# Tiles 6 and 7 split on ScalarE and VectorE, first logits two steps later, a fourth staging place for the second weight matrix

## The chip, the cores and the metric

One core of one Trainium2 chip runs the whole program. The metric is the device time of one execution in microseconds (us). The engines are named as in the profile: PE (matmul), PEld (weight load), DVE (VectorE), ACT (ScalarE), POOL (GpSimd), SP (SyncE, which here only issues transfers; its queue is SPq).

## The reference, cut to what matters

```python
x = attention(q, k, v)               # 4 batches, 8 heads, 768 positions, head size 64; ALiBi bias,
                                     # window of 96 positions plus 8 global ones, softmax
x = x.transpose(0, 2, 1, 3).reshape(3072, 512)
h = x @ w_in                         # 512 -> 2048
x = (h * sigmoid(h)) @ w_out         # 2048 -> 512
logits = x @ phi                     # 512 -> 32 slots
d = softmax(logits, axis=0)          # over the 3072 tokens
slot_out = relu((d.T @ x) @ w1) @ w2 # 8 experts, 4 slots each
out = softmax(logits, axis=1) @ slot_out
```

The weights `w_in` and `w_out` arrive as 64-bit words and are narrowed on the chip.

## The kernel before, in words

The 3072 tokens are 24 tiles of 128, and three tiles make a chunk (8 chunks). Matmuls run in float16 with each operand split into a high and a low half (`hi`, line 196, writes the rounded high half; `lo`, line 206, the remainder), so a product takes three matmuls. A `hi` on ACT or POOL is a copy with scale (L200, L202). A `lo` is a subtraction of two SBUF operands on DVE or POOL (L208) or a scaled one on DVE (L210).

Attention of a tile T is `load` (its q, k, v), `split` (hi and lo of q, k and v), four `s_step` (two heads each: scores by L316 or L326, bias and minimum by L331 on DVE, exp by L332 on ACT; after the second and the fourth, the probabilities of four heads are split and transposed by a DMA, L349) and two `pv_step` (L371, normalization L382 to L384, split and transposition of the result, L394). Tiles 0 to 5 are "paired": their q and k are used in float32, and only v and the probabilities are split. Tiles 6 and up split q, k and v as well. Which engine does a `hi` is read from strings indexed by tile: `HE` (q, k, v) and `PHE` (probabilities), and `PLE` for the `lo` of the probabilities; a tile beyond the string's end takes POOL for these. Loads of q, k and v of tiles 6 and up go through one staging set, `stage_m`, so the load of tile T+1 waits until the split of tile T has read it.

The dense part of a chunk is 16 `l1_step` (12 matmuls L503 to L505, tanh on ACT L507, gate on DVE L509, hi on ACT and lo on DVE) and, for the chunk's three tiles, the second product (L523 to L525) into three PSUM banks, `l2_end` (hi, lo and a DMA transposition L536) and `logits` (L545, then L547 to L551), queued a number of steps later by `at`. A "step" is one call of `slot_end`, about one `l1_step`. While chunk c is worked on, the attention items of the next chunk's tiles are dealt out over its steps: chunk 0 runs beside the attention of tiles 3 to 5 and the beginning of tile 6, with the splits of tiles 6, 7 and 8.

The weights come in 16 pieces of 1 MB, 0 to 7 of `w_in` and 8 to 15 of `w_out`. `w_ahead` (line 447) issues the load of the next piece as soon as its place in `place` is free; `conv` (line 454) narrows a piece and splits it: L461 on ACT, L463 on DVE, a check by two matmuls L468 (and L470 on ACT for every second piece), L471 on DVE, hi L481 on ACT, lo L489 on DVE; then its place is free. Pieces 10 to 15 are converted inside the second product of chunk 0, which needs piece 8 + i for its steps 2i and 2i + 1. The place of piece 11 is that of 8, of 12 that of 9, of 13 that of 10, of 14 that of 11, of 15 that of 12.

The text of the program is the priority order from which a scheduler makes each engine's fixed order; an engine, and SPq too, works strictly in its order.

Of the kernel before, what the change touches and what calls it, by code (L numbers as in the profile page):

```python
# [81 lines left out]

START = [3, 9, 14, 18, 22, 99, 99, 99]
AHEAD = [0, 0, 0, 0, 0, 5, 8, 11, 13, 15]
HE = 'AAAAAA'
PHE = 'AAAAAA'
PLE = 'VVVVVV'
LOE = 'VVVVVVVVVVVVVVVV'
BE = 'P'
NPAIR = 6  # L90
# [4 lines left out]
GATE = {1: (0, 0), 2: (0, 1), 3: (1, 0), 4: (1, 1), 5: (2, 0), 6: (2, 1)}  # L95
# [5 lines left out]
def fast_kernel(tc, keepp, q_l, k_l, v_l, q_f, k_f, n_global, n_local, w_in, w_out, phi, w1, w2, shapes, pick_c, out):  # L101
# [8 lines left out]
    with ExitStack() as ctx:  # L110
# [129 lines left out]
        def at(lag, fn):  # L240
            seq[0] += 1
            heapq.heappush(heap, (now[0] + lag, seq[0], fn))
# [195 lines left out]

        wq = [wo0 + 8192 * i for i in range(4)]
        we = [ext0, ext0 + 8192]  # L440
        place = [wq[0], wq[1], wq[2], wq[3], we[0], we[1], wq[0], wq[1], we[0], we[1], wq[3], we[0], we[1], wq[3], we[0], we[1]]
        holder = {}
        nload = [0]

        done_p = set()

        def w_ahead():
            while nload[0] < 16 and holder.get(place[nload[0]]) is None and (GATE.get(nload[0]) is None or GATE[nload[0]] in done_p):
                p = nload[0]
                holder[place[p]] = p  # L450
                nc.sync.dma_start(out=ar.view(place[p], [2048], I32), in_=(w_in if p < 8 else w_out)[p % 8].bitcast(I32))
                nload[0] += 1
# [74 lines left out]
        def l2_end(c, m):  # L527
            op = bW[(turn[0] + m) % 4]
            T = first[c] + m
            xh, xtr = x2hl[m], x2t[T % 3]  # L530
            hi("A", xh[:, 0], op, E_X2 - E_G - E_WO)
            lo("V", xh[:, 1], op, E_X2 - E_G - E_WO, xh[:, 0])
            if m == 0:
                absmax(6 + 2 * c, xh[:, 0, 0:128])
                absmax(7 + 2 * c, g_of[CHUNKS[c]][:, 15, 0, 0:128])
            nc.sync.dma_start_transpose(out=xtr, in_=xh.rearrange("p z f -> p (z f)"))  # L536
            at(6 if c == 0 else CFG["lag_l"], lambda: logits(c, m))


        def logits(c, m):  # L540
# [290 lines left out]
        for c in range(NCH):  # L831
# [11 lines left out]
                    st["d"] += 1  # L843

            for f in range(16):
                while nconv < len(AHEAD) and AHEAD[nconv] <= f:
                    conv(nconv)
                    nconv += 1
                l1_step(c, f)
                slot_end()  # L850
                if c == NCH - 1 and 1 <= f < 11:
                    w1_halves(1, False)
                elif c == NCH - 1 and f >= 14:
                    w1_halves(1)
            if c == NCH - 1:
# [12 lines left out]
                g_slot = [[g0 + 8192 * i for i in range(3) if min(4, -(-8192 * (i + 1) // (4 * per_f))) == q + 1] for q in range(4)]  # L868
                g_slot[3] += [g0 + 8192 * i for i in range(3) if 8192 * (i + 1) > 16 * per_f and g0 + 8192 * i not in g_slot[3]]
            if c == 0:  # L870
                for f in range(0, 16, 2):
                    if nconv < 16:
                        conv(nconv)
                        nconv += 1
                    for m in range(n):
                        l2_part(c, m, range(f, f + 2))
                    slot_end()
                    if f % 4 == 2:
                        slot_end()

                V.tensor_reduce(out=odd, in_=oddp, axis=AX.X, op=ALU.max)
                G.memset(acc, 0.0)
                G.memset(ssum, 0.0)
                G.memset(mrun[0], -3e38)
                absmax(4, wih[:, 0, 0, 0:128])
                absmax(5, woh[:, 0, 0, 0:128])
                absmax(NSMP - 1, phi16[:, :, 0], AX.XY)
                for m in range(n):
                    l2_end(c, m)
                    tick()  # L890
            elif c == NCH - 1:
                while heap:
                    tick()
                last_begin(c)
                pick = ar.view(ls0 + 512, [2, NS], F32)
                nc.sync.dma_start(out=pick, in_=pick_c.rearrange("p (s o c) -> p s o c", s=2, o=4)[:, :, 0])
                for q in range(3):
                    for f in range(4 * q, 4 * q + 4):
                        for j in range(4):
                            last_part(c, j, (f,))  # L900
                        w1_halves(1 + (f % 4 < 2))
                    w_units([wo0 + 8192 * q] + g_slot[q])
                for j in range(4):
                    last_part(c, j, range(12, 16))
                    last_end(c, j)
                    if j < 3:
                        last_turn(c, j)
                    if j in (1, 2):
                        w1_halves(1)
                w_units([home[1, 15]])  # L910
                for u in range(16):
                    home[1, u] = moved[u]
            else:
                for m in range(n):
                    for q in range(4):
                        l2_part(c, m, range(4 * q, 4 * q + 4))
                        if q == 3:
                            l2_end(c, m)
                        slot_end()
# [464 lines left out]
```

## Time and profile before

| what | value |
|---|---|
| median of 3 runs | 723.83 us (721.11 to 727.09) |
| profiled execution | 723.92 us |
| its span, first to last instruction | 722.1 us |
| PE busy | 672.4 us (93%), 5175 matmuls |
| DVE busy | 500.4 us (69%) |
| ACT busy | 357.3 us (49%) |
| POOL busy | 252.4 us (35%) |
| mean granted PE clock | 0.98 of full |

Busy shares are means over stages. A row of the timeline gives start, duration, engine, line, operation, output and inputs, and in brackets the idle time of that engine just before with what ended it. Matmul durations overlap, so their pace is read from start to start.

### The profile page before, as it was taken

The page shows a single profiled execution, that of the slowest core. Times are in us where ns is not written, and L with a number is a line of the kernel's source. Part 1 is how long each engine was busy: PE and PEld are TensorE (multiplying, and loading weights), DVE is VectorE, ACT ScalarE, POOL GpSimd, SP SyncE. Part 2 cuts the span into 40 slices and gives each one's busy share as a digit, 9 for nine tenths or more (in the row PEclk, how much of TensorE's full clock was granted, in tenths as well). Part 3 has the DMA queues.
Part 4 walks back from the last instruction along what each step waited for, and adds up shares of the span by engine and source line. Part 5 has one row for each costly group of instructions (what it writes and reads, how often), then busy time and mean ns, then how long its engine had stood idle before and what let it go on. Part 6 is the DMA issues. An engine that isn't in the chain of part 4 may idle for free.

```text
span 722.1 us, 13677 instructions
## 1 busy us (share of the span) xinstructions
PE 672.4 (93%) x5175; PEld 387.1 (54%) x5175; DVE 500.4 (69%) x1189; ACT 357.3 (49%) x902; POOL 252.4 (35%) x211
## 2 busy tenths in 40 slices
PE   4779989789999999999999999999999989999992
PEld 2445534346655665566556655665566536665552
DVE  4999998977854877387638873876386158797432
ACT  5678766436522553265235533652266147574322
POOL 3110103423552566235625662356143400190000
PEclk9989998999999999999999999999999999999997
DMA  7999657672482567536645566355424893196998
GB/s 222 242 296 265 188 153 236 182 174 59 118 161 59 117 133 167 96 80 123 141 84 117 121 156 118 74 119 116 74 42 65 200 293 106 61 369 241 389 401 293
DMA packets 165257, 120.08 MB, mean 166 GB/s; under 512 B 143936, under 2 KB 150464, under 8 KB 159168
## 3 DMA queue, kind: packets, MB, share of 16 engines
q1 hardware_dynamic: 163968, 118.15, 62.2%
q10 hardware_dynamic: 1216, 0.99, 0.4%
q8 instruction: 42, 0.69, 0.4%
q14 instruction: 31, 0.25, 0.1%
HBM read 79.01 MB, written 6.29 MB: 118 GB/s over the span
## 4 chain that ended last, share of the span: by engine, by line


## 5 line engine op out<-in xcount | busy, mean ns | idle before, releaser
L202 POOL TENSOR_SCALAR arena<-arena 128x1024 f16<-128x1024 f32 (+5 forms) x115 | 118.1, 1038 | 293.4 <-ACT arena L332 112.8
L503 PE MATMUL bank<-rows,arena 128*128 128x384 f16 x512 | 167.9, 329 | 0.0
L505 PE MATMUL bank<-rows,arena 128*128 128x384 f16 x512 | 167.7, 328 | 0.0
L504 PE MATMUL bank<-rows,arena 128*128 128x384 f16 x512 | 167.7, 328 | 0.0
L200 ACT ACTIVATE arena<-bank 128x384 f16<-128x384 f32 (+1 forms) x153 | 77.2, 505 | 156.4 <-DVE bank L509 92.5
L332 ACT ACTIVATE arena<-arena 128x256 f32<-128x256 f32 (+1 forms) x192 | 92.4, 482 | 86.8 <-DVE arena L331 85.6
L524 PE MATMUL bank<-arena 128*128 128x512 f16 x336 | 128.6, 383 | 2.3 <-DVE arena L489 2.3
L525 PE MATMUL bank<-arena 128*128 128x512 f16 x336 | 128.6, 383 | 0.0
L523 PE MATMUL bank<-arena 128*128 128x512 f16 x336 | 127.3, 384 | 0.5 <-DVE arena L210 0.5
L210 DVE SCALAR_TENSOR_TENSOR arena<-bank,arena 128x384 f16<-128x384 f32 (+2 forms) x154 | 87.6, 570 | 27.3 <-ACT arena L200 26.3
L208 POOL TENSOR_TENSOR arena<-arena 128x1024 f16<-128x1024 f32 (+1 forms) x45 | 93.4, 2077 | 25.1 <-ACT arena L200 22.1
L331 DVE CUSTOM_DVE_ANT_0 arena<-bank,arena 128x256 f32<-128x256 f32 (+1 forms) x192 | 70.3, 394 | 33.7 <-PE bank L326 29.8
L509 DVE SCALAR_TENSOR_TENSOR bank<-arena,bank 128x384 f32<-128x384 f32 x128 | 71.0, 558 | 26.3 <-ACT arena L507 25.3
L208 DVE TENSOR_TENSOR arena<-arena 128x1024 f16<-128x1024 f32 (+2 forms) x50 | 68.9, 1378 | 13.1 <-POOL arena L202 12.4
L210 DVE SCALAR_TENSOR_TENSOR arena<-arena 128x1024 f16<-128x1024 f32 (+3 forms) x64 | 66.7, 1057 | 8.8 <-POOL arena L202 5.7
L505 PEld LDWEIGHTS <-arena 128*128 128x128 f16 x512 | 50.3, 98 | 33.7 <-issue 0.7
L503 PEld LDWEIGHTS <-arena 128*128 128x128 f16 x512 | 50.2, 98 | 33.3 <-issue 5.6
L507 ACT ACTIVATE arena<-bank 128x384 f32<-128x384 f32 x128 | 61.5, 481 | 12.3 <-PE bank L505 11.5
L504 PEld LDWEIGHTS <-arena 128*128 128x128 f16 x512 | 50.3, 98 | 28.1 <-issue 0.7
L200 ACT ACTIVATE arena<-arena 128x1024 f16<-128x1024 f32 (+1 forms) x61 | 55.4, 913 | 15.3 <-DVE arena L210 8.2
L525 PEld LDWEIGHTS <-arena 128*128 128x128 f16 x336 | 33.1, 98 | 41.8 <-issue 3.6
L524 PEld LDWEIGHTS <-arena 128*128 128x128 f16 x336 | 33.2, 99 | 36.7 <-issue 3.5
(185 smaller groups left out, 817.1 us busy)
## 6 DMA issues: line engine op xcount, KB each, us to landing
arena<-in_w_dram SPq DMA_DIRECT2D x31, 1024.0 KB, 8.6
arena<-in_q_l_dram SPq DMA_DIRECT2D x18, 512.0 KB, 3.7
arena<-in_k_l_dram SPq DMA_DIRECT2D x18, 512.0 KB, 4.3
arena<-in_w_in_dram SPq DMA_DIRECT2D x8, 1024.0 KB, 6.0
arena<-in_w_out_dram SPq DMA_DIRECT2D x8, 1024.0 KB, 5.4
arena<-in_v_l_dram SPq DMA_DIRECT2D x24, 256.0 KB, 3.1
out_dram<-arena SPq DMA_DIRECT2D x4, 768.0 KB, 8.1
arena<-in_q_f_dram SPq DMA_DIRECT2D x6, 256.0 KB, 5.1
```

Source lines behind the costliest of these rows:

```text
L200: A.activation(out=out, in_=in_, func=AF.Copy, scale=p2(e))
L202: G.tensor_scalar(out=out, in0=in_, scalar1=p2(e), scalar2=0.0, op0=ALU.mult, op1=ALU.add)
L208: (V if eng == "V" else G).tensor_tensor(out=out, in0=in_, in1=h, op=ALU.subtract)
L210: return V.scalar_tensor_tensor(out=out, in0=in_, scalar=p2(e), in1=h, op0=ALU.mult, op1=ALU.subtract)
L332: A.activation(out=pw, in_=pw, func=AF.Exp, scale=-1.0, bias=nmx[:, T, h:h + 1], accum_out=psum_[T % 2][:, h:h + 1])
L503: mm(hp, wh, x[:, 0, k], start=(k == 0), stop=False)
L504: mm(hp, wh, x[:, 1, k], start=False, stop=False)
L505: mm(hp, wl, x[:, 0, k], start=False, stop=(k == 3))
L509: gated.append(V.scalar_tensor_tensor(out=hp, in0=th, scalar=1.0, in1=hp, op0=ALU.add, op1=ALU.mult))
L523: mm(op, gh, woh[:, f, 0], start=(f == 0), stop=False)
L524: mm(op, gh, woh[:, f, 1], start=False, stop=False)
L525: mm(op, gl, woh[:, f, 0], start=False, stop=(f == 15))
```

## The change

It makes four edits. `HE` becomes 8 long and `PHE` and `PLE` 7: the hi of q, k and v of tiles 6 and 7 and the hi of tile 6's probabilities go from POOL to ACT, the lo of tile 6's probabilities from POOL to DVE. In `l2_end`, the logits of chunk 0 are queued 8 steps later instead of 6. In `place`, piece 9 goes to `wq[2]`, and the pieces after it use the four places `we[0]`, `we[1]`, `wq[2]`, `wq[3]`: piece 11 takes the place of 5, 12 that of 8, 13 that of 10, 14 that of 11, 15 that of 12. And `most` bounds the pieces loaded: 9 at first, one more before steps 3, 5, 7, 9 and 11 of chunk 0, and all from its second product on.

```diff
-HE = 'AAAAAA'
-PHE = 'AAAAAA'
-PLE = 'VVVVVV'
+HE = 'AAAAAAAA'
+PHE = 'AAAAAAA'
+PLE = 'VVVVVVV'
...
-        place = [wq[0], wq[1], wq[2], wq[3], we[0], we[1], wq[0], wq[1], we[0], we[1], wq[3], we[0], we[1], wq[3], we[0], we[1]]
+        place = [wq[0], wq[1], wq[2], wq[3], we[0], we[1], wq[0], wq[1], we[0], wq[2], wq[3], we[1], we[0], wq[3], we[1], we[0]]
...
-        nload = [0]
+        nload, most = [0], [9]
...
-            while nload[0] < 16 and holder.get(place[nload[0]]) is None and (GATE.get(nload[0]) is None or GATE[nload[0]] in done_p):
+            while nload[0] < most[0] and holder.get(place[nload[0]]) is None and (GATE.get(nload[0]) is None or GATE[nload[0]] in done_p):
...
-            at(6 if c == 0 else CFG["lag_l"], lambda: logits(c, m))
+            at(8 if c == 0 else CFG["lag_l"], lambda: logits(c, m))
...
             for f in range(16):
+                if c == 0 and f in (3, 5, 7, 9, 11):
+                    most[0] += 1
+                    w_ahead()
...
             if c == 0:
+                most[0] = 16
```

The scheduler rebuilds every engine's order from about the sixth `l1_step` of chunk 0 to the middle of chunk 1; behind that the orders are the same. Three places matter below. The first is SPq at the end of chunk 0. In the kernel before (L451 loads pieces 14 and 15; L268 loads q, k, v of tile 8, then q and k of tile 9; the two L349 of 128x8x128 transpose tile 6's probabilities):

```order
L451 DMA arena<-in_w_out_dram 128x2048
L349 DMA_TRANSPOSE arena<-arena 128x16x128
L268 DMA arena<-in_q_l_dram 128x1024
L451 DMA arena<-in_w_out_dram 128x2048
L349 DMA_TRANSPOSE arena<-arena 128x8x128
L268 DMA arena<-in_k_l_dram 128x1024
L268 DMA arena<-in_v_l_dram 128x512
L394 DMA_TRANSPOSE rows<-arena 128x8x128
L268 DMA arena<-in_q_l_dram 128x1024
L349 DMA_TRANSPOSE arena<-arena 128x8x128
L268 DMA arena<-in_k_l_dram 128x1024
```

In the changed kernel, from piece 14 to the first transpositions of `l2_end` (L536):

```order
L451 DMA arena<-in_w_out_dram 128x2048
L349 DMA_TRANSPOSE arena<-arena 128x16x128
L451 DMA arena<-in_w_out_dram 128x2048
L349 DMA_TRANSPOSE arena<-arena 128x8x128
L268 DMA arena<-in_q_l_dram 128x1024
L268 DMA arena<-in_k_l_dram 128x1024
L268 DMA arena<-in_v_l_dram 128x512
L394 DMA_TRANSPOSE rows<-arena 128x8x128
L268 DMA arena<-in_k_l_dram 128x1024
L268 DMA arena<-in_v_l_dram 128x512
L536 DMA_TRANSPOSE arena<-arena 128x8x128 x2
```

The load of tile 9's k now stands right behind tile 5's last transposition (L394) and ahead of the L536, and the second transposition of tile 6's probabilities, which stood ahead of it, is behind the L536.

The second place is ACT in the first steps of the second product. Before (L461 and L481 are conversions, L332 the exp of tile 5):

```order
L332 ACTIVATE arena<-arena 128x256 x2
L481 ACTIVATE arena<-arena 128x2x512
L470 ACTIVATE arena<-bank_77 128x512
L332 ACTIVATE arena<-arena 128x256
L461 ACTIVATE arena<-arena 128x1024
```

In the changed kernel (the three L200 are the hi of q, k and v of tile 7, the two L481 are pieces 10 and 11):

```order
L332 ACTIVATE arena<-arena 128x256 x2
L200 ACTIVATE arena<-arena 128x1024
L200 ACTIVATE arena<-arena 128x8x128
L200 ACTIVATE arena<-arena 128x8x64
L470 ACTIVATE arena<-bank_77 128x512
L481 ACTIVATE arena<-arena 128x2x512 x2
```

Three hi of tile 7 now stand in front of the check of piece 11 and of the hi of pieces 10 and 11.

The third place is DVE around the last conversion. Before (L489 is the lo of piece 15, L208 of 64x1024 the lo of tile 8's q, the two L208 of 128x8x128 the lo of k of tiles 8 and 9, the L210 from banks 73 to 75 the lo of `l2_end`, L509 the first gate of chunk 1):

```order
L331 ISA arena<-bank_71,arena 128x128
L331 ISA arena 128x1
L208 TENSOR_TENSOR arena<-arena 64x1024
L489 SCALAR_TENSOR_TENSOR arena<-arena 128x2x512
L208 TENSOR_TENSOR arena<-arena 128x8x128
...
L210 SCALAR_TENSOR_TENSOR arena<-bank_74,arena 128x512
L210 SCALAR_TENSOR_TENSOR arena<-bank_75,arena 128x512
L208 TENSOR_TENSOR arena<-arena 128x8x128
L509 SCALAR_TENSOR_TENSOR bank_76<-arena,bank_76 128x384
```

In the changed kernel:

```order
L208 TENSOR_TENSOR arena<-arena 128x8x128
L489 SCALAR_TENSOR_TENSOR arena<-arena 128x2x512
...
L210 SCALAR_TENSOR_TENSOR arena<-bank_74,arena 128x512
L208 TENSOR_TENSOR arena<-arena 128x8x128
L210 SCALAR_TENSOR_TENSOR arena<-bank_75,arena 128x512
L210 SCALAR_TENSOR_TENSOR arena<-arena 128x8x64
L509 SCALAR_TENSOR_TENSOR bank_76<-arena,bank_76 128x384
L331 ISA arena<-bank_71,arena 128x128
L331 ISA arena 128x1
L331 ISA arena<-bank_71,arena 128x128
L331 ISA arena 128x1
L208 TENSOR_TENSOR arena<-arena 64x1024
```

Two scores of tile 6 (L331 from bank 71) and the lo of tile 8's q went behind the last conversion and behind chunk 1's first gate; the lo of tile 8's k went ahead of the conversion, and that of tile 9's k ahead of the third lo of `l2_end`.

## Rows read from the trace of the kernel before

**Rows 1.** Busy time by stretch: busy us (instructions) per engine, PE clock, DMA, GB/s.

```profile
100.85:151.40 50.55, 44.28 (x256) 19.51 (x255) 48.34 (x73) 26.52 (x56) 18.34 (x12) 0.93 0.71 208
109.20:115.60 6.40, 6.40 (x16) 2.17 (x16) 6.40 (x11) 2.17 (x6) 3.71 (x2) 0.50 0.77 273
162.65:170.00 7.35, 7.35 (x50) 4.35 (x50) 4.58 (x17) 4.88 (x16) 3.18 (x2) 0.77 0.12 38
170.00:231.00 61.00, 61.00 (x469) 35.32 (x467) 36.98 (x98) 24.64 (x73) 26.40 (x20) 1.00 0.52 110
```

**Rows 2.** Waits of PE, 100 to 170 us: total, times, longest.

```profile
PE bank L545 <- DVE arena L548: 2.7, 1, 2.7
PE bank L524 <- DVE arena L489: 2.3, 3, 1.5
PE bank L468 <- DVE arena L463: 1.7, 3, 0.8
PE bank L316 <- DVE arena L331: 1.7, 1, 1.7
PE bank L523 <- DVE arena L210: 0.5, 1, 0.5
```

**Rows 3.** Timeline of DVE: instructions with two SBUF inputs, two plain ones first.

```profile
89.51 0.68 DVE L208 TENSOR_TENSOR arena<-arena 128x512 f16<-128x512 f32 x1
146.58 1.23 DVE L489 SCALAR_TENSOR_TENSOR arena<-arena 128x1024 f16<-128x1024 f32 x1
...
96.02 2.06 DVE L208 TENSOR_TENSOR arena<-arena 128x1024 f16<-128x1024 f32 x1
113.53 1.78 DVE L489 SCALAR_TENSOR_TENSOR arena<-arena 128x1024 f16<-128x1024 f32 x1
128.56 1.52 DVE L489 SCALAR_TENSOR_TENSOR arena<-arena 128x1024 f16<-128x1024 f32 x1
130.00 2.17 DVE L471 SCALAR_TENSOR_TENSOR arena<-arena 128x1024 int32<-128x1024 int32 x1
133.23 1.52 DVE L210 SCALAR_TENSOR_TENSOR arena<-arena 128x512 f16<-128x512 f32 x1
```

**Rows 4.** Timeline of POOL in chunk 0.

```profile
129.09 2.00 POOL L208 TENSOR_TENSOR arena<-arena 128x512 f16<-128x512 f32 x1
132.11 2.11 POOL L202 TENSOR_SCALAR arena<-arena 128x1024 f16<-128x1024 f32 x1 [1.01 <-DMA arena<-in_q_l_dram]
```

**Rows 5.** Timeline of DVE: its idle times between 75 and 147 us.

```profile
80.24 1.35 DVE L463 TENSOR_SCALAR arena<-arena 128x1024 uint16<-128x1024 uint16 x1 [1.03 <-ACT arena L461]
94.53 0.42 DVE L331 CUSTOM_DVE_ANT_0 arena<-bank,arena 128x256 f32<-128x256 f32 x1 [0.78 <-PE bank L316]
117.16 1.72 DVE L471 SCALAR_TENSOR_TENSOR arena<-arena 128x1024 int32<-128x1024 int32 x1 [1.25 <-PE bank L468]
119.93 0.69 DVE L208 TENSOR_TENSOR rows<-arena,rows 128x512 f16<-128x512 f32 x1 [0.50 <-ACT rows L200]
```

**Rows 6.** Timelines of SPq, DVE and PE at the start of chunk 1.

```profile
150.40 1.23 SPq L349 DMA_TRANSPOSE arena<-arena  x1
151.72 0.53 SPq L268 DMA_DIRECT2D arena<-in_k_l_dram  x1
...
157.37 1.23 DVE L208 TENSOR_TENSOR arena<-arena 128x1024 f16<-128x1024 f32 x1 [4.00 <-POOL arena L202]
161.24 0.19 DVE L547 TENSOR_SCALAR arena<-bank 128x32 f32<-128x32 f32 x1
...
162.65 0.38 PE L545 MATMUL bank<-arena 128*128 128x64 f16 x8 [2.67 <-DVE arena L548]
```

**Rows 7.** Timeline of ACT in chunk 0: two hi and a conversion's hi.

```profile
87.88 0.63 ACT L200 ACTIVATE arena<-arena 128x512 f16<-128x512 f32 x1
93.97 1.04 ACT L200 ACTIVATE arena<-arena 128x1024 f16<-128x1024 f32 x1
111.76 1.15 ACT L481 ACTIVATE arena<-arena 128x1024 f16<-128x1024 f32 x1 [1.53 <-DVE arena L471]
```

## The prediction

> **What bounds the kernel now.** I read the busy times by stretch first. From 170 us on, PE runs without a gap for the next 61 us at full clock, and from the middle of chunk 1, soon behind that point, the changed kernel's orders are those of before. So the change can only gain or lose up to about 170 us, and whatever it does there arrives at the end unshortened. In the second product of chunk 0 (100.85 to 151.40 us) DVE is busy for 48.3 of 50.6 us and PE for 44.3, at a granted clock of 0.93 [rows 1]: DVE sets the pace and PE waits for it.
>
> Next, the waits of PE between 100 and 170 us. All five groups name DVE: conversions (L489 and L463, 2.3 and 1.7 us), scores (L331, 1.7), a gate (0.5), and one wait of 2.7 for the first tile's logits (L548); 8.9 us together [rows 2]. Two of them were followed by a slow clock. From 109.2 to 115.6 us the granted clock is 0.50, the lower level of 1.2 GHz, which costs half of 6.4 = 3.2 us of PE's time. From 162.65 to 170 us it averages 0.77, costing 0.23 x 7.35 = 1.7 us [rows 1]. With everything at its best, 8.9 + 3.2 + 1.7 = 13.8 us are to be had.
>
> Third, why DVE is late in chunk 0. Its instructions with two SBUF inputs stretch while POOL works: 512 elements take 0.68 us alone, and the L210 of 133.23 us takes 1.52 beside POOL's L202 of 132.11; 1024 elements take 1.23 us alone, and the L471 of 130.00 us takes 2.17 beside POOL's L208 of 129.09 [rows 3, 4]. The latter ends about its own plain length after POOL's: 132.17 against 129.09 + 2.00 = 131.09.
>
> Fourth, the 2.7 us wait. SPq works in order. The load of tile 9's k was issued only at 151.72, behind the transposition of tile 6's probabilities at 150.40; DVE then stood still for 4.00 us in front of the lo of that k, and the logits' L547 came at 161.24 [rows 6]. PE, ready at 160.0, got its bank at 162.65 [rows 6].
>
> **The change, part by part.** The yardstick is the end of the last conversion (L489 of piece 15, 146.58 + 1.23 = 147.8 us [rows 3]), since the second product ends some 3.5 us behind it.
>
> *Contention removed.* POOL loses the hi of q, k, v of tiles 6 and 7 and both splits of tile 6's probabilities, and the hi of tile 8's q moves behind the last conversion. The DVE rows stretched by exactly these, against 1.22 plain (0.68 for L210): 2.06 - 1.22 = 0.84; 1.78 - 1.22 = 0.56; 1.52 - 1.22 = 0.30; 2.17 - 1.22 = 0.95; 1.52 - 0.68 = 0.84 [rows 3]. Sum 3.5 us.
>
> *Work added on DVE.* Of tile 6's two lo, one falls ahead of the last conversion: 0.60 from start to start (0.68 long [rows 3]). The other falls in chunk 1, where DVE has room (busy 4.58 of the 7.35 us from 162.65 [rows 1]); I cost it at nothing, and 0.6 if that room is gone.
>
> *Rows that cross the last conversion.* Two scores (0.42 together) and the lo of tile 8's q (1.2) go behind it, the lo of tile 8's k (1.2) comes ahead. Net gain 0.4 us. DVE work is thus shorter by 3.5 - 0.6 + 0.4 = 3.3 us.
>
> *Idle times of DVE.* There are 1.03, 0.78, 1.25 and 0.50 us [rows 5], 3.6 together. The first is the conversion of piece 10 waiting for its load; with the new order of conversions that L463 stands far later, so the 1.03 go. The 1.25 is DVE waiting for a check matmul that PE ran in its half-clock stretch. Bounds are 0 and 3.6; I take 1.7, the first and half of the third. The sum to the last conversion is 3.3 + 1.7 = 5.0 us, with bounds 3.3 and 6.9. PE can follow, since it has 6.2 us of waits and 3.2 of half clock to give there.
>
> *The staging place.* Pieces 11 and 12 are loaded one conversion earlier, no bytes are added, and pieces 13 to 15 wait for the same conversions as before. The loads are hidden already behind DVE's lateness, so nothing beyond the 1.03 is booked. If the cover goes (conversions catch up with the loads of 14 and 15), it shows as waits of ACT's L461 for a load.
>
> *Work added on ACT.* Seven hi ahead of chunk 1, each 1.04 (128x1024) or 0.63 us (128x512) [rows 7]: 2 x (1.04 + 1.04 + 0.63) + 0.63 = 6.1 us, beside 26.5 busy of 50.6 us [rows 1]. There is room, but ACT works in order. Queued behind the hi of tile 7's q, which must wait for PE's last score of tile 5, are the check of piece 11 and the hi of pieces 10 and 11; DVE's L489 and SPq's loads of 13 and 14 wait for those. I cost this at nothing, because those conversions need an L463 and an L471 each on DVE first, which cover the 2.7 us.
>
> *Logits later, tile 9's k earlier.* The load of k no longer stands behind tile 6's transposition. And the first logits matmul comes two steps later, at 12 matmuls of 0.163 us plus attention about 2.4 us a step, so 4.8 us, while PE's next logits matmul waited for DVE by 2.7 us [rows 6]. The wait of 2.7 us and its half clock of 1.7 should go: at most 4.4, at least 0. A wait in front of tile 9's k stays likely, shorter (it now delays the third `l2_end`), so I take 3.5.
>
> **The sum.** 723.9 - 5.0 - 3.5 = 715.4 us, against the profiled execution's 723.92, which lies 0.1 us over the median.
>
> One rule of the Trainium skill speaks against the move between the two vector engines. The trace says of tile 6's first probabilities: POOL's pair stretched DVE's L489 and L471 by 0.30 + 0.95 = 1.25 us, and the lo costs DVE 0.60 when it does it itself [rows 3]. "Perfetto Trace Analysis", section Optimizing Scalar/DVE Operations, holds that shifting work between GpSimd and VectorE might not help, since they share a read port. By the page the 0.65 would be nil and the sum 716.1; by the rows it stands.
>
> **The rivals.** *PE takes only part.* New waits appear between ACT and DVE in the reordered stretch, and DVE waits once more for PE. Then the idle times stay, ACT's extra 2.7 us of hi of tile 6 in its fullest stretch delay a conversion by 1 to 2 us, and the logits' half is gained: 3.3 - 1.5 + 1.8 = 3.6 us, so 720.3. For it: ACT's order is fixed and its hi sit between conversions; against it: ACT is idle nearly half of the stretch.
>
> *All waits go.* 6.9 + 4.4 = 11.3 us gives 712.6, and a PE that no longer waits at all (13.8) gives 710.1. Against it: DVE has hardly any slack in the stretch [rows 1], so it can't give PE more than its own gain.
>
> *Slower.* In front of the hi of tile 7's q, ACT waits for PE's score, with 1.04 + 1.04 + 0.63 = 2.7 us of hi and two conversions of 1.15 [rows 7] queued: 5.0 us by which the lo of pieces 10 and 11 can slip. The loads of 13 and 14 are tied to them, so the slip runs through to the last conversion; PE's waits grow by as much and another half-clock stretch costs 3.2. The shorter work of DVE counts for nothing then, since DVE idles, and the logits gain nothing: 723.9 + 5.0 + 3.2 = 732.1. It decides where the hi of q begins after DVE has finished piece 11's L471; by the present rows the score is out before that.
>
> *The change does nothing.* The waits on conversions remain because the place chain of 12 to 15 is what it was, and the logits' wait comes back at the new place: 723 to 724. The DVE rows speak against it, since the stretching has to vanish with POOL's work.
>
> **How the numbers follow.** My forecast has a chance of 0.52 (its own range 712.5 to 719), the part gain 0.24, all waits 0.10, slower 0.08, nothing 0.06. A measurement of this kernel can tell about 1% from no change, 7.2 us, so "faster" begins below 716.6. From the forecast 0.38 lies below that, with the 0.10 of the larger gain 0.48; "slower" begins above 731.1, where nearly all of the slower case lies, 0.07; 0.45 is the rest. The range for 8 in 10 runs from 711 to 722.5: it leaves out the slower case, the nothing case and the far end of the larger gain.
>
> **What would show it.** In the changed profile, DVE's L471, L489, L208 and L210 in the second product of chunk 0 should run at 1.22 and 0.68 us; the second product should end near 146 us instead of 151; PE's waits between 100 and 165 us should fall from 8.9 us to 3 or 4 without L545 among them; and from chunk 1 on, everything is the same but some 8 us earlier. I would be wrong if ACT idles in front of an L200 of 128x1024 while an L489 is wanted, if the clock falls again in the second product, if DVE stands for several us in front of tile 9's k, or if PE waits for a new line in chunk 1.

## The result: 717.25 us, and the profile after

| what | before | after |
|---|---|---|
| median | 725.46 us (721.11 to 727.19, 4 runs) | 717.25 us (714.40 to 718.77, 4 runs) |
| ratio, 95% interval | | 0.9895 (0.9854 to 0.9936) |
| profiled execution, its span | 723.92, 722.1 us | 718.77, 717.0 us |
| PE, DVE, ACT, POOL busy (us) | 672, 500, 357, 252 | 669, 498, 363, 241 |
| granted PE clock, mean | 0.98 | 0.987 |

The changed kernel is faster by 1.05%. Six further runs of it (below) had a median of 714.90; all ten together 715.6.

To say where, I cut the span at three events on the chip: chunk 0's first L503 on PE, the start of the last L525 of chunk 0's second product on PE, and chunk 1's first L547 on DVE. **Stretch A** lies between the first two, **stretch B** between the last two. Behind B, and ahead of A, every engine's order is the same in all kernels here. In the busy times by stretch (us; then busy us and instructions of PE, PEld, DVE, ACT, POOL; granted PE clock, DMA share, GB/s) A and B of before are

```profile
52.96:150.88 97.92, 89.81 (x562) 43.48 (x561) 93.08 (x164) 64.63 (x142) 22.16 (x17) 0.96 0.70 202
150.88:218.19 67.31, 64.58 (x517) 38.68 (x516) 46.86 (x126) 31.61 (x92) 30.96 (x23) 0.97 0.58 126
```

and of after

```profile
52.96:149.51 96.55, 88.03 (x555) 43.39 (x555) 88.62 (x164) 69.32 (x145) 8.59 (x7) 0.97 0.75 208
149.51:212.47 62.96, 62.96 (x521) 38.43 (x520) 48.65 (x129) 32.97 (x97) 32.74 (x24) 1.00 0.61 131
```

A is shorter by 1.4 us, B by 4.35: together 5.7, of which the rest of the span gives 0.6 back. In B, PE now works without a gap at full clock. In A, DVE's work fell by 93.08 - 88.62 = 4.5 us, but its idle time rose from 97.92 - 93.08 = 4.8 to 96.55 - 88.62 = 7.9 us. These are two single profiles; how far A differs between two executions of one order is seen below, in b_logits.

**B** is what the prediction's last part spoke of. After's timelines of SPq, DVE and PE, which answer to [rows 6]:

```profile
145.34 0.33 SPq L268 DMA_DIRECT2D arena<-in_k_l_dram  x1
149.12 2.62 SPq L536 DMA_TRANSPOSE arena<-arena  x2
...
150.09 1.22 DVE L208 TENSOR_TENSOR arena<-arena 128x1024 f16<-128x1024 f32 x1
161.13 0.19 DVE L547 TENSOR_SCALAR arena<-bank 128x32 f32<-128x32 f32 x1 [0.24 <-PE bank L545]
...
160.71 0.38 PE L545 MATMUL bank<-arena 128*128 128x64 f16 x8
162.88 0.38 PE L545 MATMUL bank<-arena 128*128 128x64 f16 x8
```

Tile 9's k is loaded at 145.34, 4.2 us ahead of the end of A. In the kernel before it was loaded at 151.72, 0.8 us behind that end and behind tile 6's transposition. DVE's lo of it at 150.09 has no idle time in front of it (4.00 us in the kernel before). The second tile's logits, the L545 at 162.88 that waited 2.67 us in the kernel before, wait for nothing, and at the first tile's (160.71) DVE waits for PE, 0.24 us.

**A** did in part what was forecast. DVE's two-operand rows and POOL's one remaining pair beside them, which answer to [rows 3, 4]:

```profile
130.77 1.22 DVE L471 SCALAR_TENSOR_TENSOR arena<-arena 128x1024 int32<-128x1024 int32 x1
131.91 1.22 DVE L208 TENSOR_TENSOR arena<-arena 128x1024 f16<-128x1024 f32 x1
133.04 0.68 DVE L210 SCALAR_TENSOR_TENSOR arena<-arena 128x512 f16<-128x512 f32 x1
139.99 1.78 DVE L489 SCALAR_TENSOR_TENSOR arena<-arena 128x1024 f16<-128x1024 f32 x1
145.23 1.21 DVE L489 SCALAR_TENSOR_TENSOR arena<-arena 128x1024 f16<-128x1024 f32 x1
...
139.65 2.60 POOL L202 TENSOR_SCALAR arena<-arena 128x1024 f16<-128x1024 f32 x2 [21.95 <-DMA arena<-in_k_l_dram]
```

They run at their plain length, but for the L489 at 139.99 beside POOL's hi of tile 8's k and v, which stay on POOL; another L489, at 117.25, still takes 1.52 us beside a POOL row that ends at 117.70. Yet the last conversion ends at 145.23 + 1.21 = 146.44, 1.4 us earlier and not 5.0. Rows from after's timelines of SPq, ACT, DVE and PE show new idle time:

```profile
71.21 2.76 SPq L349 DMA_TRANSPOSE arena<-arena  x1
74.01 0.58 SPq L265 DMA_DIRECT2D arena<-in_v_l_dram  x1
...
78.06 0.63 ACT L200 ACTIVATE arena<-arena 128x512 f16<-128x512 f32 x1 [2.75 <-DMA arena<-in_v_l_dram]
...
79.10 0.56 DVE L509 SCALAR_TENSOR_TENSOR bank<-arena,bank 128x384 f32<-128x384 f32 x1 [1.99 <-ACT arena L507]
100.66 1.23 DVE L489 SCALAR_TENSOR_TENSOR arena<-arena 128x1024 f16<-128x1024 f32 x1 [1.05 <-ACT arena L481]
...
91.93 0.99 PE L316 MATMUL bank<-arena 64*128 64x256 f32 x4 [2.39 <-issue]
```

Three things are seen. Tile 5's v is loaded at 74.01, behind a transposition (65.81 in the kernel before, ahead of it); ACT stands 2.75 us before its hi, the tanh L507 is queued behind that, and DVE waits 1.99 us for it. PE stands 2.39 us before two scores of tile 5, which now stand ahead of tile 4's second `pv_step`. And before the L481 on which DVE waits 1.05 us, ACT does a hi of tile 6 that was POOL's. The waits of PE between 100 and 170 us, which answer to [rows 2], are

```profile
PE bank L468 <- DVE arena L463: 1.8, 3, 0.7
PE bank L316 <- DVE arena L331: 1.3, 1, 1.3
PE bank L524 <- DVE arena L489: 1.0, 2, 0.8
PE bank L523 <- ACT arena L481: 0.7, 1, 0.7
PE bank L468 <- DVE arena L383: 0.6, 1, 0.6
```

5.4 us in all instead of 8.9; L545's 2.7 is gone, L523 now waits for ACT.

### The profile page after: what moved, and what is told of

Its sections match the earlier page's. It is cut to its first block, busy times and chain, and to the rows that moved or that the text cites. A ratio compares the mean times of both kernels' runs of the same rounds, so it can differ in the third digit from the quotient of the medians.

```text
span 717.0 us, 13665 instructions
## 1 busy us (share of the span) xinstructions
PE 669.4 (93%) x5175; PEld 387.1 (54%) x5175; DVE 497.6 (69%) x1191; ACT 363.2 (51%) x910; POOL 240.6 (34%) x201
## 4 chain that ended last, share of the span: by engine, by line
## 5 line engine op out<-in xcount | busy, mean ns | idle before, releaser
L202 POOL TENSOR_SCALAR arena<-arena 128x1024 f16<-128x1024 f32 (+4 forms) x107 | 110.2, 1040 | 299.9 <-ACT arena L332 100.5
L503 PE MATMUL bank<-rows,arena 128*128 128x384 f16 x512 | 168.2, 329 | 0.3 <-ACT rows L200 0.3
L200 ACT ACTIVATE arena<-bank 128x384 f16<-128x384 f32 (+1 forms) x153 | 77.3, 505 | 149.9 <-DVE bank L509 85.8
L332 ACT ACTIVATE arena<-arena 128x256 f32<-128x256 f32 (+1 forms) x192 | 92.4, 482 | 84.8 <-DVE arena L331 83.6
L525 PE MATMUL bank<-arena 128*128 128x512 f16 x336 | 127.6, 380 | 0.0
L523 PE MATMUL bank<-arena 128*128 128x512 f16 x336 | 126.6, 381 | 0.7 <-ACT arena L481 0.7
L210 DVE SCALAR_TENSOR_TENSOR arena<-bank,arena 128x384 f16<-128x384 f32 (+2 forms) x154 | 87.7, 570 | 29.5 <-ACT arena L200 28.7
L208 POOL TENSOR_TENSOR arena<-arena 128x1024 f16<-128x1024 f32 (+1 forms) x43 | 89.4, 2080 | 25.4 <-ACT arena L200 22.5
L331 DVE CUSTOM_DVE_ANT_0 arena<-bank,arena 128x256 f32<-128x256 f32 (+1 forms) x192 | 70.2, 394 | 30.9 <-PE bank L326 27.7
L509 DVE SCALAR_TENSOR_TENSOR bank<-arena,bank 128x384 f32<-128x384 f32 x128 | 71.2, 558 | 29.2 <-ACT arena L507 28.2
L208 DVE TENSOR_TENSOR arena<-arena 128x1024 f16<-128x1024 f32 (+2 forms) x52 | 69.4, 1334 | 9.9 <-POOL arena L202 8.8
L200 ACT ACTIVATE arena<-arena 128x1024 f16<-128x1024 f32 (+1 forms) x69 | 62.0, 904 | 19.6 <-DVE arena L210 8.4
L210 DVE SCALAR_TENSOR_TENSOR arena<-arena 128x1024 f16<-128x1024 f32 (+3 forms) x64 | 64.2, 1017 | 7.3 <-POOL arena L202 4.2
L503 PEld LDWEIGHTS <-arena 128*128 128x128 f16 x512 | 50.5, 99 | 33.2 <-issue 5.0
L507 ACT ACTIVATE arena<-bank 128x384 f32<-128x384 f32 x128 | 61.6, 481 | 12.3 <-PE bank L505 11.5
L525 PEld LDWEIGHTS <-arena 128*128 128x128 f16 x336 | 33.0, 98 | 41.9 <-issue 3.6
L523 PEld LDWEIGHTS <-arena 128*128 128x128 f16 x336 | 32.8, 98 | 36.2 <-issue 2.6
```

The costliest lines, as they stand in the source:

```text
L200: A.activation(out=out, in_=in_, func=AF.Copy, scale=p2(e))
L202: G.tensor_scalar(out=out, in0=in_, scalar1=p2(e), scalar2=0.0, op0=ALU.mult, op1=ALU.add)
L208: (V if eng == "V" else G).tensor_tensor(out=out, in0=in_, in1=h, op=ALU.subtract)
L210: return V.scalar_tensor_tensor(out=out, in0=in_, scalar=p2(e), in1=h, op0=ALU.mult, op1=ALU.subtract)
L332: A.activation(out=pw, in_=pw, func=AF.Exp, scale=-1.0, bias=nmx[:, T, h:h + 1], accum_out=psum_[T % 2][:, h:h + 1])
L503: mm(hp, wh, x[:, 0, k], start=(k == 0), stop=False)
```

## The experiments

Theory: the splits earn in A, an earlier tile 9's k earns in B, and the staging edit with its late v (of tile 5) and early scores takes part of A back. Rivals: all of the gain comes from the later logits; ACT's seven hi eat what the splits earn; the new idle times of A cost nothing. The table has every run; A, B and the rest of the span are from its one profile, the time is the median of its runs, and the ratio is against runs of the kernel before taken beside them, 74 in all.

| kernel | time (runs) | ratio, 95% interval | A | B | rest |
|---|---|---|---|---|---|
| before | 724.2 (74) | | 97.9 | 67.3 | 556.9 |
| b_split | 717.70 (6) | 0.9898 (0.9851 to 0.9945) | 96.1 | 66.3 | 557.4 |
| b_logits | 723.28 (12) | 0.9977 (0.9956 to 0.9997) | 102.3 | 65.3 | 557.0 |
| b_stage | 721.32 (12) | 0.9950 (0.9925 to 0.9975) | 98.6 | 63.2 | 557.7 |
| a_nostage | 721.93 (12) | 0.9954 (0.9929 to 0.9979) | 95.9 | 67.2 | 558.5 |
| after_again | 714.90 (6) | 0.9878 (0.9852 to 0.9904) | 95.7 | 63.0 | 554.6 |
| a_lag6 | 716.92 (6) | 0.9891 (0.9866 to 0.9916) | 97.7 | 63.8 | 557.5 |
| n_lo9 | 721.03 (12) | 0.9958 (0.9935 to 0.9980) | 95.0 | 69.0 | 556.2 |
| m56_lo9 | 721.28 (10) | 0.9959 (0.9935 to 0.9983) | 95.5 | 67.9 | 555.0 |
| v_early | 717.01 (6) | 0.9895 (0.9869 to 0.9922) | 96.4 | 63.4 | 560.3 |
| s_behind | 715.60 (4) | 0.9874 (0.9847 to 0.9901) | 96.0 | 63.4 | 556.1 |
| both | 717.59 (5) | 0.9907 (0.9884 to 0.9930) | 96.8 | 63.4 | 555.6 |
| a_nosplit | 719.76 (8) | 0.9943 (0.9920 to 0.9966) | 98.5 | 64.1 | 555.1 |

The rest, where nothing is changed, varies by 5.7 us from profile to profile; A and B are what the edits show in, and the medians of many runs. In A several kernels have the very same order on every engine: before and b_logits 97.9 and 102.3 us; b_stage and a_nosplit 98.6 and 98.5; b_split, a_nostage and n_lo9 96.1, 95.9 and 95.0; after, after_again and a_lag6 96.55, 95.7 and 97.7. Differences of A within these groups are chance.

**b_split: the splits alone, on the kernel before.**

```diff
-HE = 'AAAAAA'
-PHE = 'AAAAAA'
-PLE = 'VVVVVV'
+HE = 'AAAAAAAA'
+PHE = 'AAAAAAA'
+PLE = 'VVVVVVV'
```

> The kernel before with the three strings of the change alone (tiles 6 and 7 split off POOL). Theory 1 (the splits earn what the prediction's DVE rows say, and the loss in chunk 0 comes from the staging edit): the stretched L471, L489, L208 and L210 of chunk 0 fall to 1.22 and 0.68 us, the last conversion ends 2 to 3.5 us earlier, PE keeps its logits wait of about 2.7: 720.5 to 722 us against 723.9. Theory 2 (the seven hi on ACT delay conversions and eat the gain): the rows shorten all the same, but DVE waits for ACT by as much and the last conversion ends within 1 us of before: 723 to 724.5.

A and B in its profile:

```profile
52.89:149.00 96.11, 89.29 (x569) 43.83 (x567) 89.11 (x171) 71.33 (x154) 7.36 (x7) 0.96 0.72 202
149.00:215.27 66.27, 64.03 (x510) 38.38 (x509) 47.53 (x123) 30.64 (x88) 30.88 (x23) 0.97 0.59 134
```

The last conversion ends at 145.92, 1.9 us earlier, just under theory 1's 2 to 3.5. DVE's work is 4.0 us less than in the profile of before (89.11), but its idle time is 96.11 - 89.11 = 7.0, so against that profile theory 2 holds for half. PE keeps its logits wait (2.24 us). The median, 717.70, lies below the ranges of both theories: three runs took 714.4 to 715.1 and three 720.3 to 721.8, and the profiled one is of the slower three. Why is open. The three other kernels with splits and without an early k of tile 9 have medians of 721.0 to 721.9. Of these a_nostage differs from b_split by the later logits alone, and their intervals overlap, so what the splits are worth by themselves is not settled by these runs.

**b_logits: the logits two steps later, alone.**

```diff
-            at(6 if c == 0 else CFG["lag_l"], lambda: logits(c, m))
+            at(8 if c == 0 else CFG["lag_l"], lambda: logits(c, m))
```

> The kernel before with the logits of chunk 0 two steps later and nothing else. Theory 1 (this edit alone covers the 2.7 us wait and saves its half clock): the L545 wait falls under 0.5 us and 162 to 170 us runs at full clock: 719.5 to 721 us against 723.9. Theory 2 (the wait goes only because the staging edit issues the load of tile 9's k earlier): DVE still stands 4 us in front of that k's lo, the L545 wait comes back later: 723 to 724.

Theory 2 by the time and the wait. On DVE and PE the wait stands where it stood, two steps on:

```profile
162.06 1.22 DVE L208 TENSOR_TENSOR arena<-arena 128x1024 f16<-128x1024 f32 x1 [3.96 <-POOL arena L202]
...
171.30 0.38 PE L545 MATMUL bank<-arena 128*128 128x64 f16 x8 [2.10 <-DVE arena L548]
```

Its A and B:

```profile
53.28:155.61 102.33, 91.86 (x561) 44.50 (x560) 95.00 (x164) 65.09 (x142) 24.88 (x17) 0.94 0.73 193
155.61:220.89 65.28, 62.95 (x517) 38.15 (x516) 47.12 (x126) 31.67 (x92) 31.18 (x23) 1.00 0.61 130
```

B is 2.0 us shorter than in before, although the wait is nearly as long: the granted clock is 1.00 in it and not 0.97. In A every engine has the order of before, and yet it took 102.3 us here against 97.9, with a granted clock of 0.94 against 0.96 and with 102.33 - 95.00 = 7.3 us of DVE idle time against 4.8: so much may A differ between two executions of one order.

**b_stage: the staging edit alone** (places and load steps as in the diff above, nothing else).

> The kernel before with the staging places and the fixed load steps alone. Theory 1 (this edit moves tile 5's load of v behind a transposition and pulls two scores of tile 5 ahead on PE, and so costs chunk 0 some 2 to 4 us): the last conversion ends 1 to 3 us later than before's 147.8 us, PE waits 2 us or more in front of L316 near 92 us; the earlier load of tile 9's k gives 2 to 4 back: 722 to 725 us. Theory 2 (staging brings the gain): the last conversion ends earlier than 147.8, 718 to 721 us.

```profile
53.24:151.83 98.59, 89.23 (x555) 43.22 (x554) 91.14 (x162) 63.56 (x137) 19.50 (x15) 0.97 0.72 202
151.83:215.00 63.17, 63.17 (x523) 38.59 (x522) 48.04 (x127) 31.58 (x96) 33.54 (x26) 1.00 0.60 130
```

These are its A and B. On SPq:

```profile
147.85 0.33 SPq L268 DMA_DIRECT2D arena<-in_k_l_dram  x1
151.00 2.62 SPq L536 DMA_TRANSPOSE arena<-arena  x2
```

Neither theory had the place right: A gains nothing (98.59; its last conversion ended earlier, at 145.64, but the second product 1 us later), while in B the logits' wait is gone with the logits still at 6 steps. Tile 9's k is loaded at 147.85, 4.0 us ahead of the end of A, and PE has no gap in B. Theory 1's waits are there, 1.99 us of DVE before the L509 at 79.64 and 2.38 of PE before the L316 at 92.46, so they come with this edit. The time, 721.32, lies between the two ranges.

**a_nostage: the change without its staging edit.**

> The changed kernel without its staging edit (places and load steps of before; splits and later logits kept). Theory 1: tile 5's v is loaded early and the scores of tile 5 stand where they stood, so neither DVE's 2.0 us in front of L509 near 79 us nor PE's 2.4 us near 92 us is there; the last conversion ends 2 to 3.5 us before 147.8, the L545 wait is gone: 714.5 to 716.5 us, 1 to 3 us better than the change. Theory 2 (the staging edit is needed for the gain): 719 to 722 us, slower than the change.

```profile
52.74:148.63 95.89, 88.88 (x567) 43.61 (x567) 89.09 (x171) 71.41 (x154) 7.14 (x7) 0.97 0.73 203
148.63:215.80 67.17, 64.19 (x510) 38.32 (x509) 48.08 (x122) 30.85 (x88) 31.20 (x23) 0.97 0.57 133
```

A and B; and rows of SPq, DVE and PE in B:

```profile
151.19 2.89 SPq L536 DMA_TRANSPOSE arena<-arena  x2
154.14 0.57 SPq L268 DMA_DIRECT2D arena<-in_k_l_dram  x1
...
159.37 1.62 DVE L208 TENSOR_TENSOR arena<-arena 128x1024 f16<-128x1024 f32 x1 [3.38 <-POOL arena L202]
...
164.54 0.40 PE L545 MATMUL bank<-arena 128*128 128x64 f16 x8 [2.98 <-DVE arena L548]
```

Theory 2, and my hope of a faster version with it: A is 0.7 us better than after's, but B is 4.2 worse. The k is loaded at 154.14, 5.5 us behind the end of A and behind the L536, DVE stands 3.38 us before its lo, and PE waits 2.98 for the logits, with the logits at 8 steps.

**after_again: the changed kernel, unchanged,** beside the next three.

> The changed kernel once more, unchanged, beside the next three. Theory 1 (the profile of after caught an execution whose early stages were slow, and much of chunk 0's loss is chance from one execution to the next): the last conversion ends at another time than 146.4 us by 1 us or more, the median is 716 to 718. Theory 2 (the late v of tile 5 and the scores pulled ahead cost the same in each execution): DVE's idle time before L509 near 79 us and PE's before L316 near 92 us are 1.5 to 2.5 us each again, the last conversion ends within 0.7 us of 146.4; median 717 to 719.

Theory 2 in its mechanism: the idle times are there again (2.68 us before the L509 at 79.12, 2.39 before the L316 at 91.94), and the last conversion ends at 145.72, 0.7 us from after's. The 2.68 is a little over the range given, and the median, 714.90, is lower than either theory had it.

**a_lag6: the change with the logits at 6 steps.**

```diff
-            at(8 if c == 0 else CFG["lag_l"], lambda: logits(c, m))
+            at(6 if c == 0 else CFG["lag_l"], lambda: logits(c, m))
```

> The changed kernel with the logits of chunk 0 back at 6 steps. Theory 1 (the wait for the logits went because the staging edit brings tile 9's k early, and the later logits add nothing): no wait on L545 over 0.5 us, time within 1 us of the changed kernel, 716 to 718.5. Theory 2 (the later logits are what removes the wait): the L545 wait of 2 to 3 us is back: 719.5 to 722 us.

```profile
160.86 0.38 PE L545 MATMUL bank<-arena 128*128 128x64 f16 x8 [0.66 <-DVE arena L548]
```

Theory 1, but for this 0.66 us: B is 63.8 against 63.0. That is what the later logits are worth in B once the k is early. The medians (716.92 and 714.90) are 2.0 us apart where theory 1 allowed 1, with overlapping intervals.

**n_lo9: without staging, tile 9's lo of q and k on POOL.**

```diff
-HLO = 'VVVVVV'
+HLO = 'VVVVVVVVVP'
```

> The changed kernel without its staging edit, and with the lo of tile 9's q and k on POOL instead of DVE, loads left as they are. Theory 1 (PE waits for the logits because DVE's order stands in front of tile 9's k, 3.4 us in the run without staging): that idle time and the L545 wait of 3.0 us go though the load is late as before; 2.5 to 4 us faster than the 721.9 us of that run: 717.5 to 719.5. Theory 2 (the logits are late for another reason, and the k only fills the time): L545 waits 2 to 3 us again: 721 to 723.

```profile
158.92 2.13 POOL L208 TENSOR_TENSOR arena<-arena 128x1024 f16<-128x1024 f32 x1
...
158.99 2.61 DVE L210 SCALAR_TENSOR_TENSOR arena<-arena 128x512 f16<-128x512 f32 x1 [2.56 <-POOL arena L202]
...
164.69 0.48 PE L545 MATMUL bank<-arena 128*128 128x64 f16 x8 [3.79 <-DVE arena L548]
```

By the numbers theory 2, but the experiment did not take the cause away. In the place of k's lo, DVE's order now has the lo of tile 9's v (L210), whose hi on POOL stands behind k's; DVE waits for the same load, 2.56 us, and the L210 then takes 2.61 beside POOL's L208, where plain it takes 0.68. PE waits longer than before.

**m56_lo9: the four places of the change, with other load steps, and with tile 9's lo as in n_lo9.**

```diff
-HLO = 'VVVVVV'
+HLO = 'VVVVVVVVVP'
...
-                if c == 0 and f in (3, 5, 7, 9, 11):
+                if c == 0 and f in (5, 6, 7, 9, 11):
```

> The changed kernel with its four staging places, but the loads at steps 5, 6, 7, 9, 11 (tile 5's v then stands ahead of piece 9 and of the transposition on the transfer queue, and its scores behind the second product of tile 4 on PE, both as in the kernel before), and the lo of tile 9's q and k on POOL. Theory 1 (late v and early scores cost chunk 0 of the changed kernel 2 to 4 us): neither idle time is there, the last conversion ends 2 to 4 us ahead of the changed kernel's: 713 to 715.5 us. Theory 2 (they lie beside other lateness): the last conversion within 1 us of the changed kernel's, 716.5 to 718.5 us.

Neither: 721.28 us. A has no late v and no early scores and is 95.5; but with these steps tile 9's k stands behind the L536 again, and B is 67.9 with an L545 wait of 3.7 us. Beside n_lo9 (721.03), which has the same lo and no staging edit, the four places with these steps bring nothing that shows. What counts in B is where the load of k comes to stand. That follows from the whole order and not from the load steps alone: v_early and both, below, have the same steps, and their k is early.

**v_early, s_behind, both: are A's new waits worth anything?** Three kernels in which tile 9's k stays early and the splits are kept. v_early has tile 5's v ahead of the transposition, s_behind the scores behind the product, both has the two. AHEAD gives the steps of conversions.

The edit of v_early on the change:

```diff
-AHEAD = [0, 0, 0, 0, 0, 5, 8, 11, 13, 15]
+AHEAD = [0, 0, 0, 0, 0, 5, 7, 11, 13, 15]
...
-                if c == 0 and f in (3, 5, 7, 9, 11):
+                if c == 0 and f in (5, 6, 7, 9, 11):
```

Of s_behind:

```diff
-AHEAD = [0, 0, 0, 0, 0, 5, 8, 11, 13, 15]
+AHEAD = [0, 0, 0, 0, 0, 6, 9, 11, 13, 15]
```

Of both, with the load steps of v_early:

```diff
-AHEAD = [0, 0, 0, 0, 0, 5, 8, 11, 13, 15]
+AHEAD = [0, 0, 0, 0, 0, 4, 8, 11, 13, 15]
```

> The changed kernel with the loads of pieces 9 and 10 at steps 5 and 6 and the conversion of piece 6 one step earlier. Its transfer queue loads tile 5's v ahead of piece 9 and of the transposition, as before the change; its PE order still has the two scores of tile 5 ahead (where the change put them), and tile 9's k is loaded early. Theory 1 (the late v costs DVE 2.0 us near 79 us, and that time reaches the last conversion): DVE's idle time before L509 near 79 us goes, the last conversion ends 1 to 2 us ahead of the changed kernel's 145.7 and 146.4; 713.5 to 715 us against 715.6 for the changed kernel's ten runs together. Theory 2 (the time is swallowed by the scores' wait near 92 us): that wait grows or stays, the last conversion within 0.5 us: 715 to 717 us.

> The changed kernel with the conversions of pieces 5 and 6 one step later. Tile 5's v is loaded late as in the change and tile 9's k early, but PE has the two scores of tile 5 behind tile 4's second product, as before the change. Theory 1 (the scores stand in front of PE's work too early: 2.4 us of waiting and a half clock behind it): the wait on L316 near 92 us falls under 0.7 us, 80 to 100 us runs at full clock, the last conversion ends 1.5 to 3 us earlier: 712.5 to 714.5 us. Theory 2 (DVE is what PE waits for there in any order): PE's idle time from 60 to 140 us stays at 8.2 us or more, 715 to 717 us.

> The changed kernel with the loads of pieces 9 and 10 at steps 5 and 6 and the conversion of piece 5 one step earlier: tile 5's v early and its scores behind, tile 9's k early. Theory 1 (the two waits of chunk 0 are what the staging edit took back): neither is there, PE idles 6 to 6.5 us from 60 to 140 us as in the runs without staging, and none of the waits on the logits returns: 711.5 to 714 us. Theory 2 (chunk 0 is set by DVE whatever the order): 8 us of idle time, 715 to 717 us.

By the times theory 2 in all three, with 717.59 (both) 0.6 us above its range: A is 96.4, 96.0 and 96.8 us against 96.55 and 95.7, and the last conversions end at 147.1, 146.7 and 146.4. In s_behind the signs that theory 1 named for PE did come, without the gain: the wait near 92 us goes, PE idles 6.3 us from 60 to 140 us instead of 8.2, and the clock is 1.00 from 80 to 100 us. What comes in its place is seen in its timelines of PE and DVE and its busy times from 100 to 120 us:

```profile
91.60 0.67 PE L316 MATMUL bank<-arena 64*128 64x256 f32 x2 [0.41 <-issue]
108.23 0.72 PE L316 MATMUL bank<-arena 64*128 64x256 f32 x2 [1.67 <-DVE arena L331]
...
114.32 1.23 DVE L471 SCALAR_TENSOR_TENSOR arena<-arena 128x1024 int32<-128x1024 int32 x1 [1.34 <-PE bank L468]
116.50 1.23 DVE L471 SCALAR_TENSOR_TENSOR arena<-arena 128x1024 int32<-128x1024 int32 x1 [0.84 <-PE bank L468]
```

```profile
100.00:120.00 20.00, 17.17 (x84) 6.52 (x83) 17.19 (x28) 12.05 (x23) 2.72 (x2) 0.83 0.60 161
```

PE waits at 108.23 instead, its clock falls there (0.83, so up to 3.4 us of 20; in after 1.00), and DVE waits 2.2 us for PE's checks. In v_early the scores still wait 2.15 us, and DVE waits for ACT for 1.36 and 1.10 us, at 78.43 and 83.56; in both, whose DVE order differs in many places, the scores wait 3.67 us at 93.54. None of the three beats the change beyond its interval.

**a_nosplit: the change without the splits.**

> The changed kernel without the splits (tiles 6 and 7 back on POOL; staging edit and later logits kept). Theory 1 (splits and staging earn in different stretches: the splits 2 to 4 us between chunk 0's first matmul and the end of its second product, the staging 3.5 to 5 us behind it): the first stretch is 98 to 100 us again (95.7 and 96.5 in the two profiles of the changed kernel), the second, to chunk 1's logits, stays at 63 to 64 us: 719 to 721.5 us. Theory 2 (the staging places alone let DVE run ahead, and the splits add nothing to that): 95.5 to 97 us in the first stretch, 715 to 717.5 us.

```profile
53.06:151.59 98.53, 87.86 (x554) 43.23 (x554) 92.67 (x163) 64.28 (x138) 19.93 (x14) 0.97 0.73 204
151.59:215.64 64.05, 63.34 (x523) 38.53 (x522) 48.34 (x128) 32.19 (x96) 34.49 (x26) 1.00 0.58 129
```

Theory 1: A is 98.5 again, B 64.1, and the time 719.76.

## Why the prediction was right or wrong

The time was right: 715.4 was forecast, 717.25 measured, 715.6 over ten runs. Against the 724.2 of before's 74 runs that is a gain of 8.6 us, and 8.5 were forecast. So close a fit is in part luck: ten runs of the changed kernel spread over 5 us, one term of the sum shows in no profile, and the term that is borne out best was expected from the wrong edit.

**Where the end is decided.** This held: from 170 us to the end of B, PE works without a gap at a granted clock of 1.00 in before, after and after_again, and A and B together fell by 5.7 and, in after_again, by 6.6 us (165.2 to 159.5 and 158.7). The yardstick, the end of the last conversion, is good for some orders only. In b_stage it ends 2.2 us earlier than in before, but PE, which has no gap behind 138.03, ends the second product 1 us later.

**Contention: right.** Its 3.5 us, less 0.6 and plus 0.4, made 3.3 us less DVE work; 4.5 was measured in after, and 87.7 to 89.1 us of DVE work in all ten profiles with splits stand against 91.1 to 95.0 in the four without. The splits earn in A: it is 97.9, 98.5, 98.6 and 102.3 us without them, 95.0 to 97.7 with them, and a_nosplit's interval (0.9920 to 0.9966) lies over after_again's (0.9852 to 0.9904). "Perfetto Trace Analysis" of the Trainium skill, section Optimizing Scalar/DVE Operations, which the prediction weighed, says that offloading operations between GpSimd and VectorE might not help. Of the splits only the lo of tile 6's probabilities is such a shift, the hi go to ACT, and no run makes it alone: whether its 0.65 us were earned is not shown.

**DVE's idle times: nothing came back.** The prediction reclaimed 1.7 of 3.6 us and had bounds of 0 and 3.6. DVE idles for 7.9 and 8.0 us of A in after and after_again, and for 6.3 at least in all ten profiles with splits; the order of before has 4.8 in one profile and 7.3 in another. So the 1.7 is in no profile. Whether idle time was added, which the bounds left out, is open, since before's own order varies by 2.5 us. For the same reason it is open how far A fell short of the 5.0: it gave 1.4 and 2.2 us against before, 5.8 and 6.6 against b_logits. The signs of the rival *PE takes only part* are there, new waits between ACT and DVE and the hi in front of L481, but its time (720.3) is not. No single wait explains A: with the late v gone, or the early scores, A stays within 0.6 us of after's 96.55, and idle time turns up at another place. What bounds A at 95 to 98 us with DVE idle for 6 to 10 of them stays open; DVE, ACT and PE hand work to each other there in fixed orders, and none is full.

**Extra hi on ACT: price open.** They were costed at nothing. In b_split, which has no staging edit, A is 1.8 us below before's with 4.0 us less DVE work, and 6.2 below b_logits's with 5.9 less; a price of some 2 us cannot be told from chance here. The slower rival (ACT stuck before tile 7's q, 732.1) came only in small: in after ACT stands 0.46 and 1.11 us before hi of tile 7, at 111.86 and 114.03, and DVE then waits 0.46 us for the L481 behind them.

**The staging edit: expected in the wrong place.** It was booked at 1.03 us in A, and that wait did go (the L463 of piece 10 is at 111.69). The sign that was named for a lost cover came too, ACT's L461 waits 1.95 us at 135.12 for the load of piece 15, but DVE begins the L463 behind it only at 138.01, so it costs nothing that shows. What the edit earns lies in B. B is 63.0 to 64.1 us in the eight profiles that load tile 9's k 3.2 to 4.2 us ahead of the end of A, and 65.3 to 69.0 in the six that load it 0.8 to 5.5 us behind it. In before and b_logits the load stood behind tile 6's transposition, in the other four behind the L536 as well. PE's longest wait before an L545 is 0 to 0.7 us in the eight and 2.1 to 3.8 in the six. No run moves this load and nothing else; n_lo9, which was to take its effect away by another road, did not. Neither edit is clearly the larger by the medians: without staging the change takes 721.93 us, without splits 719.76, with overlapping intervals.

**Logits: size nearly right, reason half right.** 3.5 was taken of at most 4.4; B gave 4.35 in both profiles. The prediction named two reasons. The two steps, "4.8 us", did not cover the wait: without an early k it is 2.1 us (b_logits) and 3.0 (a_nostage), because DVE's order has the lo of tile 9's k ahead of the logits' first operation at 8 steps too. In b_logits the two steps did take 2.0 us off B, by the clock; between b_split and a_nostage, which differ by them alone, B rose by 0.9. The other reason, the load that no longer stands behind a transposition, is the one that the fourteen profiles bear out, and it belongs to the staging edit. With it, the two steps are worth 0.8 us of B.

**What would show it.** Plain lengths: yes, but for the two L489 above and an L208 of 512 elements at 141.69 (1.09). The second product ending near 146: no, 149.5. PE's waits at 3 or 4 us: no, 5.4, though without L545. Some 8 us earlier from chunk 1 on: 5.7 at the end of B, 6.45 in after_again. The clock falling in the second product: no, 1.00 from 100 to 150 us; it fell ahead of it, to a mean of 0.91 from 80 to 100 us, where it was 1.00 in before. DVE in front of tile 9's k, or PE waiting for a new line in chunk 1: no.

## What to carry to other kernels

When an edit changes the order of a transfer queue, follow each load that moved to the first instruction that needs it, and see what is queued behind that on its engine; here a load 6 us earlier went with 4.35 us less in B, as much as the splits took off DVE's work. Before a difference of a few us in one stretch is read as the price of an edit, profile one order twice: here the same order gave 97.9 and 102.3 us for A, more than most edits changed it. And removing one wait among engines that feed each other is tested by the end of the stretch, not by the wait.

## What the runs showed of the hardware that was not expected

A low clock can be free. The orders of b_split and b_stage are the same up to 62 us. From 40 to 60 us, in b_split and in b_stage:

```profile
40.00:60.00 20.00, 15.95 (x106) 9.47 (x105) 18.50 (x36) 14.81 (x31) 1.56 (x2) 0.66 0.99 302
```

```profile
40.00:60.00 20.00, 16.23 (x103) 9.51 (x102) 18.21 (x35) 14.40 (x30) 2.73 (x3) 1.00 1.00 306
```

The granted clock averages 0.66 in one and 1.00 in the other, with DMA at 0.99 and 1.00, and chunk 0's first matmul began at 52.89 and 53.24 us. In b_split the clock was 0.50 from 45 to 53 us, ahead of that matmul, and it came no later for it. And the cost of POOL beside DVE depends on the pairing: an L210 of 512 elements on DVE took 0.68 us alone, 1.52 beside a hi on POOL [rows 3, 4], and 2.61 beside a lo (n_lo9).
